# Gated layer of a fused attention and expert kernel: one of its seven outer products made by halves, inner products in sequence, some gates on ScalarE

## The chip, the cores and the metric

The kernel runs on one core of a Trainium2 chip. The metric is the device time of one execution in microseconds (us). The core has five engines that run side by side and wait for one another through semaphores: TensorE (PE in the profile; its weight loads are PEld), VectorE (DVE), ScalarE (ACT), GpSimd (POOL) and SyncE (SP). Every engine takes its own instructions in the order in which the program gives them.

## What is computed

The reference is an attention in which a query sees only the keys of its own hash bucket, followed by a two-layer block with a squared ReLU:

```python
batch, n_heads, seq, head_dim = (4, 8, 768, 64)
q_bits = (einsum('bhsd,dk->bhsk', q, proj) > 0)      # 6 bits; the same for k
mask = q_bucket[:, :, :, None] == k_bucket[:, :, None, :]
scores = where(mask, scale * q @ k.T, -1e9)
attn_out = softmax(scores) @ v
x = attn_out.transpose(0, 2, 1, 3).reshape(3072, 512)
h = x @ w_in                      # w_in 512 x 2048
r = maximum(h, 0.0)
g = r * r
out = g @ w_out                   # w_out 2048 x 512
```

Everything is float32. The change is in the two-layer block, above all in `h = x @ w_in` and the gate `g = max(h, 0) * h`.

## The kernel before

The block works on three chunks of 1024 rows (`NCHUNK` = 3). Both of its matrix products are made with Strassen's scheme in Winograd's form: each operand is cut into 2 x 2 blocks, and seven products of half-size blocks take the place of eight. `product` is that scheme for one block of weights. The weights' sums are kept in DRAM (`w_in_7`, and for the second level `w_in_49` and `w_out_49`); the sums of `x` are made on VectorE:

```python
def product(n, w, at, bt, c11, c12, c21, c22, hook=None):
    acc = [ps_m.tile([P, 512], FP32, name=f"acc{i}")[:, 0:w] for i in range(3)]
    ...
    add(0, at(0), bt["11"], True, False)
    one = keep(0, "one")              # ScalarE copy out of PSUM
    add(1, at(1), bt["21"], True, True)
    if hook:
        hook()
    c11(acc[1], one)
    add(0, at(4), bt["t2"], False, False)
    two = keep(0, "two")
    add(2, at(3), bt["t1"], True, False)
    five = keep(2, "five")
    add(0, at(5), bt["t3"], False, False)
    three = keep(0, "three")
    add(2, at(6), bt["22"], False, True)
    c12(acc[2], two)
    c22(three, five)
    add(0, at(2), bt["t4"], False, True)
    c21(acc[0])
```

An accumulator keeps adding after it has been copied, so the next product into the same bank must wait until the copy has been read out. `ps_m` has two buffers of each name (`acc0`, `acc1`, `acc2`) and `ps_t` has one (`acc3`, and `tp`)[...].

The first layer is made by `hidden` in chunk 0 (seven products, no second level) and by `hidden_pair` in chunks 1 and 2. A pair is two hidden units; each call of `hidden_pair` makes one half of it. Five of the seven outer products (each 128 x 512, over two blocks of features) are made whole in each half. The other two are made for both halves at once by a second level of the scheme, in seven inner products of 128 x 256 each, spread over the call in four steps:

```python
def hidden_pair(i, n, half):
    ...
    if half == 0:
        load_inner(i, n + 1)
        now[0], now[1] = (inner_steps(i, n, j) for j in range(2))
    *steps, put = now[half]
    add(0, 0, "11", True, False)
    one = keep(0, "one")
    if half:
        now[0][4](1, b11[:, r], one)
    else:
        steps[0]()
    add(2, 3, "t1", True, False)
    five = keep(2, "five")
    steps[1 - half]()
    add(0, 4, "t2", False, False)
    two = keep(0, "two")
    steps[2 - half]()
    if half == 0:
        put(0, b11[:, r], one)
    add(2, 6, "22", False, True)
    gate_sum(b12[:, r], acc[2], two)
    steps[3 - half]()
    if half:
        put(0, b21[:, n], now["three"])
    add(0, 5, "t3", False, True)
    three = keep(0, "three")
    gate_sum(b22[:, r], three, five)
    if half:
        steps[3]()
        put(1, b21[:, r], three)
    now["three"] = three
```

`gate_sum` and `put` are an addition and a gate on VectorE; the gate is one instruction (`max(h, 0) * h`). After each half come `minus(b_t[:, r], b12[:, r], b11[:, r])`, part of the sums that the second layer starts with (`inner_sums`), `minus(b12[:, r], b22[:, r], b12[:, r])`, and two maxima over `q` and `k` (`peak`).

The second layer, `project(i)`, makes seven outer products, each by seven inner ones. Before an inner product can use `t4`, a subtraction on VectorE must have made it in place. In chunk 0, four of the steps also make the second-level weights for the first layer of the later chunks, and the first of them loads the next chunk's `x` afterwards:

```python
def factor_units(n):
    src = [new_h()... for _ in range(2)]
    for j in range(2):
        nc.gpsimd.dma_start(out=src[j], in_=w_in_7[j * NQ + n, :, 5:7])
    sums = [new_h()... for _ in range(2)]
    sums_a(...)                       # four operations on VectorE
    for lo, hi, t in (...):
        nc.gpsimd.dma_start(out=w_in_49[n, :, :, lo:hi], in_=t)

for k in range(7):                    # in project(i)
    if i == 0 and k < NQ:
        factor_units(k)
    if k == 6 and more:
        load_inner(i + 1, 0)
    def hook():
        y21 = b[:, NQ:NR, 0:QN]
        minus(y21, y21, t2)           # t4
        if k + 1 < 7 and k not in (1, 3):
            inner_sums(k + 1)
        if k == 6 and more:
            sums_inner(i + 1)
    ...
    product(NQ, QN, a_with_load, bt, ..., hook)
    if k == 0 and i + 1 < NCHUNK:
        load_x(i + 1)                 # 2 MB, on GpSimd's queue
```

`new_h` turns through five buffers.

Of the kernel before, what the change touches and what calls it, by code (L numbers as in the profile page):

```python
# [34 lines left out]
def kernel(  # L35
# [10 lines left out]
    nc = tc.nc  # L46
# [37 lines left out]

    w_in_49 = p_d.tile([NQ, P, 2, 7, P], FP32, name="w_in_49")
    w_in_21 = p_d.tile([P, NFT // 2, HF], FP32, name="w_in_21")
# [419 lines left out]

    PLACE = 0, 5, 6, 1, 2, 3, 4

    def sums_a(a11, a12, a21, a22, s1, s2, s3, s4):
        nc.vector.tensor_tensor(out=s1, in0=a21, in1=a22, op=ALU.add)  # L510
        nc.vector.tensor_tensor(out=s3, in0=a11, in1=a21, op=ALU.subtract)
        nc.vector.tensor_tensor(out=s2, in0=s1, in1=a11, op=ALU.subtract)
        nc.vector.tensor_tensor(out=s4, in0=a12, in1=s2, op=ALU.subtract)

# [49 lines left out]
    def load_unit(n, pool=p_i):  # L564

        if n < NCHUNK * NR and n not in w_unit:
            r = order(n)
            w_unit[n] = pool.tile([P, 7, NFT // 2, P], FP32, name="w_unit", bufs=2 if pool is p_i else 1)
            m = 7 if n < NR else 5
            nc.sync.dma_start(out=w_unit[n][:, 0:m], in_=w_in_7[r, :, 0:m])  # L570

    def sum_x(i, n):
# [19 lines left out]
    with tc.manual_schedule():  # L592
# [173 lines left out]
        def guard():  # L766

            most = p_k.tile([1, 2], FP32, name="most")
            tp = ps_t.tile([P, 512], FP32, name="tp")
            for w in range(2):  # L770
                nc.tensor.transpose(
                    out=tp[0:1, w * P:(w + 1) * P], in_=top[:, w:w + 1], identity=ident
                )
            nc.vector.tensor_reduce(
                out=most, in_=tp[0:1, 0:2 * P].rearrange("o (w f) -> o w f", w=2), axis=AXL.X,
                op=ALU.max,
            )
            nc.vector.tensor_scalar(
                out=slow, in0=most[:, 0:1], scalar1=most[:, 1:2], scalar2=PLAIN / (scale * D),
                op0=ALU.mult, op1=ALU.is_gt,  # L780
            )
# [51 lines left out]
        def factor_units(n):  # L833

            src = [new_h().rearrange("p (a f c) -> p a f c", a=2, c=P) for _ in range(2)]
            for j in range(2):
                nc.gpsimd.dma_start(out=src[j], in_=w_in_7[j * NQ + n, :, 5:7])
            sums = [new_h().rearrange("p (a f c) -> p a f c", a=2, c=P) for _ in range(2)]
            sums_a(
# [3 lines left out]
            for lo, hi, t in (  # L843
                (0, 2, src[0]), (2, 3, src[1][:, :, 1:2]), (3, 5, sums[0]), (5, 7, sums[1])
            ):
                nc.gpsimd.dma_start(out=w_in_49[n, :, :, lo:hi], in_=t)

        def load_inner(i, n):

            if n < NQ:  # L850
                w_inner[i, n] = []
                for j, name in enumerate((("sum0", "sum3"), ("sum2", "sum1"))[n % 2]):
                    t = p_y.tile([P, 4, QN], FP32, name=name).rearrange("p a (b c) -> p (a b) c", c=P)
                    nc.sync.dma_start(out=t[:, 0:7], in_=w_in_49[n, :, j])
                    w_inner[i, n].append(t)

        def quarters_x(i, j):

            b = xs[i][0][:, 2:4, 0:HN] if j == 0 else xs[i][0][:, 0:2, HN:NCH]
            return b[:, 0, 0:QN], b[:, 0, QN:HN], b[:, 1, 0:QN], b[:, 1, QN:HN]  # L860

        def sums_inner(i):

            t_inner[i] = [p_y.tile([P, NQ, QN], FP32, name=f"t{m}", bufs=2) for m in range(2)]
            for j, t in enumerate(t_inner[i]):
                y11, y12, y21, y22 = quarters_x(i, j)
                minus(t[:, 0], y12, y11)
                minus(t[:, 1], y22, t[:, 0])
                minus(t[:, 2], y21, t[:, 1])
                minus(y12, y22, y12)  # L870

        def inner_steps(i, n, j):


            w, t = w_inner[i, n][j], t_inner[i][j]
            y11, t3, y21, y22 = quarters_x(i, j)
            hs = {}
            if i not in snaps:
# [4 lines left out]
            def mul(out, a, b, start, stop):  # L883
                nc.tensor.matmul(  # L884
                    out=out, lhsT=w[:, a], rhs=b, start=start, stop=stop, skip_group_check=True
                )

            def step_0():
                a0, a1 = (ps_m.tile([P, 512], FP32, name="acc1")[:, 0:QN] for _ in range(2))
                mul(a0, 0, y11, True, False)  # L890
                nc.scalar.copy(out=one, in_=a0)
                mul(a1, 1, y21, True, True)
                hs[0] = new_h()
                nc.vector.tensor_tensor(out=hs[0][:, 0:QN], in0=a1, in1=one, op=ALU.add)
                hs["a0"] = a0

            def step_1():
                hs["a2"] = ps_t.tile([P, 512], FP32, name="acc3")[:, 0:QN]
                mul(hs["a0"], 4, t[:, 1], False, False)
                nc.scalar.copy(out=two, in_=hs["a0"])  # L900
                mul(hs["a2"], 3, t[:, 0], True, False)
                nc.scalar.copy(out=five, in_=hs["a2"])

            def step_2():
                mul(hs["a0"], 5, t3, False, False)
                nc.scalar.copy(out=three, in_=hs["a0"])
                mul(hs["a2"], 6, y22, False, True)
                nc.vector.tensor_tensor(out=hs[0][:, QN:HN], in0=hs["a2"], in1=two, op=ALU.add)
                hs[1] = new_h()
                nc.vector.tensor_tensor(out=hs[1][:, QN:HN], in0=three, in1=five, op=ALU.add)  # L910

            def step_3():
                mul(hs["a0"], 2, t[:, 2], False, True)
                nc.scalar.copy(out=hs[1][:, 0:QN], in_=hs["a0"])

            def put(unit, out, other):
                h = hs[unit]
                nc.vector.tensor_tensor(out=h, in0=h, in1=other, op=ALU.add)
                gated(out, h)

            return step_0, step_1, step_2, step_3, put

        def hidden_pair(i, n, half):
# [4 lines left out]

            def add(to, a, b, first, last):
                for f in range(NFT // 2):  # L930
# [5 lines left out]

            def keep(of, name):
                t = p_r.tile([P, 512], FP32, name=name)
                nc.scalar.copy(out=t, in_=acc[of])
                return t  # L940

            if half == 0:
                load_inner(i, n + 1)
                now[0], now[1] = (inner_steps(i, n, j) for j in range(2))
            *steps, put = now[half]
            add(0, 0, "11", True, False)
            one = keep(0, "one")
            if half:
                now[0][4](1, b11[:, r], one)
            else:  # L950
                steps[0]()
            add(2, 3, "t1", True, False)
            five = keep(2, "five")
            steps[1 - half]()
            add(0, 4, "t2", False, False)
            two = keep(0, "two")
            steps[2 - half]()
            if half == 0:
                put(0, b11[:, r], one)
            add(2, 6, "22", False, True)  # L960
            gate_sum(b12[:, r], acc[2], two)
            steps[3 - half]()
            if half:
                put(0, b21[:, n], now["three"])
            add(0, 5, "t3", False, True)
            three = keep(0, "three")
            gate_sum(b22[:, r], three, five)
            if half:
                steps[3]()
                put(1, b21[:, r], three)  # L970
            now["three"] = three

# [4 lines left out]

        def inner_sums(k, n=slice(0, NQ)):

# [5 lines left out]
            y11, y12, y21, y22 = b[:, n, 0:QN], b[:, n, QN:HN], b[:, at, 0:QN], b[:, at, QN:HN]  # L985
            minus(t1, y12, y11)
            minus(t2, y22, t1)
            minus(y12, y22, y12)

# [64 lines left out]
        def project(i):  # L1054
# [60 lines left out]
            for k in range(7):  # L1115
                b = OUTER[k][1]
                t1, t2 = tens.pop(k)
                if i == 0 and k < NQ:
                    factor_units(k)
                if k == 6 and more:  # L1120
                    load_inner(i + 1, 0)
                at = lambda m, k=k: lambda n: leaves[k, m][:, n]
                bt = {
# [88 lines left out]
        for i in range(NCHUNK):  # L1212
            for s in range(NR):
# [3 lines left out]
                else:  # L1217
                    hidden_pair(i, s // 2, s % 2)
                minus(b_t[:, r], b12[:, r], b11[:, r])
                if i == 0 and r in WHEN:  # L1220
# [15 lines left out]
                if i > 0 and s % 2:  # L1236
                    inner_sums(0, slice(s // 2, s // 2 + 1))
                minus(b12[:, r], b22[:, r], b12[:, r])
                for n in range(2):
# [244 lines left out]
```

## Time and profile before

| | |
|---|---|
| device time, median of 3 | 879.97 us (879.5 to 882.57) |
| span of the profiled run | 877.9 us, 12130 instructions |
| granted TensorE clock, mean | 0.996 |
| attention (to the first product of the block) | 331 us |
| chunk 0: both layers | 331 to 513 us |
| chunk 1: first layer, second layer | 513 to 606, 606 to 691 us |
| chunk 2: first layer, second layer | 691 to 784, 784 us to the end |
| one gate, 128 x 512, on VectorE (96 of them) | 691 ns |
| one addition of 128 x 512, of 128 x 256, on VectorE | 685, about 420 ns |
| one copy out of PSUM of 128 x 512, of 128 x 256, on ScalarE | 585, about 375 ns |

The profile gives each engine's busy time, groups of equal instructions with the mean length of one and the idle time just before them, and the order of time of each engine with what ended a wait. "`<-PE acc L931`" after a number of us is a wait that a product of line 931 ended. Line numbers are those of the kernel before. A float32 matmul shows as two records on TensorE, so the counts there are twice those of the code. The ends of TensorE's records are modelled; the distance from one start to the next is what a product takes.

### The profile page before, as it was taken

How to read it: one execution, taken by the hardware profiler on the slowest of the kernel's cores; microseconds unless marked ns; L12 is line 12 of the kernel's file. 1: busy time of each engine (PE TensorE's matmuls, PEld its weight loads, DVE VectorE, ACT ScalarE, POOL GpSimd, SP SyncE). 2: the span in 40 equal slices, each digit the busy share in tenths (PEclk: the TensorE clock that was granted, in tenths of full speed). 3: DMA queues.
4: the chain of work that ended last, by engine and by line, in shares of the span. 5: the costliest groups of instructions: out<-in, count | busy, mean ns of one | idle time of the engine just before them, and what ended most of it. 6: DMA issues, size and time to landing. Idle time of an engine off the chain costs nothing.

```text
span 877.9 us, 12130 instructions
## 1 busy us (share of the span) xinstructions
PE 864.8 (99%) x4340; PEld 518.7 (59%) x4340; DVE 760.4 (87%) x1099; ACT 391.5 (45%) x673; POOL 107.0 (12%) x172
## 2 busy tenths in 40 slices
PE   8999999999999999999999999999999999999996
PEld 3444444444444444444688865556888755568885
DVE  5999999999999998888779968888889788888875
ACT  6988888888888852222211123332111233321110
POOL 2000000000000001554231011111000211110002
PEclk9999999999999999999999999999999999999998
DMA  9777967998788536999897764536756754355565
GB/s 176 142 149 134 233 153 156 188 253 225 179 176 225 156 105 213 299 267 283 292 353 239 181 160 168 173 118 222 285 151 187 167 165 155 124 167 154 158 175 105
DMA packets 224131, 167.09 MB, mean 190 GB/s; under 512 B 164448, under 2 KB 181344, under 8 KB 224064
## 3 DMA queue, kind: packets, MB, share of 16 engines
q1 hardware_dynamic: 189152, 87.19, 41.0%
q0 software_dynamic: 12528, 41.30, 15.2%
q10 hardware_dynamic: 22384, 37.76, 14.0%
q8 instruction: 36, 0.59, 0.3%
q14 instruction: 31, 0.25, 0.1%
HBM read 124.52 MB, written 41.68 MB: 189 GB/s over the span
## 4 chain that ended last, share of the span: by engine, by line
PE 95%; DVE 2%; ACT 1%; DMA 1%; issue 0%; ACTq 0%; DVEq 0%
PE acc L712 40%; PE st L396 17%; PE acc L931 16%; PE xo L438 14%; PE acc L884 6%; PE hash L346 2%; PE tot L455 1%; DVE total L428 1%; DMA k_nat<-in_k_dram 1%; ACT bits L356 1%; ACT e L413 0%; PE xo L477 0%; DVE x_t L493 0%; PE tp L309 0%; DVE recs L487 0%
## 5 line engine op out<-in xcount | busy, mean ns | idle before, releaser
L413 ACT ACTIVATE e<-st 128x1024 f32<-128x1024 f32 x192 | 145.1, 810 | 44.9 <-PE st L396 41.0
L396 PE MATMUL st<-feat,feat 64*128 64x512 f32 (+1 forms) x768 | 150.4, 483 | 0.0
L438 PE MATMUL xo<-e,v_nat 128*64 128x512 f32 (+1 forms) x768 | 134.8, 492 | 0.0
L712 PE MATMUL acc<-b,leaf 128*128 128x256 f32 x600 | 133.2, 379 | 0.7 <-issue 0.7
L712 PEld LDWEIGHTS acc<-b,leaf 128*128 128x128 f32 x600 | 113.8, 190 | 17.1 <-issue 1.7
L428 DVE TENSOR_TENSOR total<-total,e 128x1536 f32<-128x1536 f32 x64 | 112.4, 1757 | 8.2 <-ACT e L413 3.6
L438 PEld LDWEIGHTS xo<-e,v_nat 128*64 128x64 f32 x768 | 51.3, 136 | 82.2 <-issue 74.3
L931 PE MATMUL acc<-t_x,w_unit 128*128 128x512 f32 x192 | 90.2, 592 | 0.0
L396 PEld LDWEIGHTS st<-feat,feat 64*128 64x128 f32 x768 | 66.0, 188 | 33.0 <-issue 23.2
L712 PE MATMUL acc<-t,leaf 128*128 128x256 f32 x336 | 76.3, 380 | 0.0
L356 ACT ACTIVATE bits<-hash,lifts 32x384 bf16<-32x384 f32 x120 | 68.6, 572 | 2.3 <-PE hash L346 0.5
L712 PEld LDWEIGHTS acc<-t,leaf 128*128 128x128 f32 x336 | 63.6, 190 | 9.4 <-DVE t L516 0.5
L796 DVE SCALAR_TENSOR_TENSOR b<-h 128x512 f32<-128x512 f32 x96 | 65.7, 691 | 3.0
L396 PE MATMUL st<-bits,bits 64*128 64x256 bf16 (+1 forms) x384 | 63.1, 325 | 1.7 <-ACT e L413 1.2
L931 PE MATMUL acc<-x,w_unit 128*128 128x512 f32 x128 | 60.1, 592 | 0.0
L712 PE MATMUL acc<-x,w_unit 128*128 128x512 f32 x128 | 56.6, 594 | 0.0
L712 PE MATMUL acc<-b_t,leaf 128*128 128x256 f32 x240 | 53.8, 379 | 0.0
L931 PEld LDWEIGHTS acc<-t_x,w_unit 128*128 128x128 f32 x192 | 36.5, 190 | 28.9 <-issue 26.8
L719 ACT COPY two<-acc 128x256 f32<-128x256 f32 (+1 forms) x29 | 12.5, 431 | 87.9 <-PE acc L712 63.1
L719 ACT COPY one<-acc 128x256 f32<-128x256 f32 (+1 forms) x29 | 12.5, 431 | 85.1 <-PE acc L712 46.9
L712 PEld LDWEIGHTS acc<-b_t,leaf 128*128 128x128 f32 x240 | 45.5, 190 | 6.2
L396 PEld LDWEIGHTS <-bits 64*128 64x128 bf16 x384 | 23.5, 93 | 42.5 <-issue 38.4
(159 smaller groups left out, 1165.5 us busy)
## 6 DMA issues: line engine op xcount, KB each, us to landing
leaf<-w_out ACTq DMA_DIRECT2D x142, 256.0 KB, 3.1
w_unit<-w_in SPq DMA_DIRECT2D x16, 640.0 KB, 4.0
raw<-in_moe_w_in_dram SPq DMA_DIRECT2D x16, 512.0 KB, 5.6
raw<-in_moe_w_out_dram SPq DMA_DIRECT2D x16, 512.0 KB, 4.6
w_unit<-w_in SPq DMA_DIRECT2D x8, 896.0 KB, 8.1
w_out<-sums POOLq DMA_DIRECT2D x16, 448.0 KB, 6.8
sum<-w_in SPq DMA_DIRECT2D x16, 448.0 KB, 4.8
v_nat<-in_v_dram SPq DMA_DIRECT2D x16, 384.0 KB, 4.3
```

Source lines behind the costliest of these rows:

```text
L346: nc.tensor.matmul(out=banks[g * NR_B:(g + 1) * NR_B, h, 0:HS], lhsT=projs[rows], rhs=feat[pr, w][rows, c * HS:(c + 1) * HS], start=True, ...
L356: nc.scalar.activation(out=t[h * D:h * D + NR_B, c * HS:(c + 1) * HS], in_=hashed[pr, w][at, h, 0:HS], func=ACTF.Sign, scale=HUGE, bias=li ...
L396: nc.tensor.matmul(out=st[:, h, 0:hi - lo], lhsT=src[pr, 1][rows, key], rhs=src[pr, 0][rows, lo:hi], start=first, stop=not first,)
L413: nc.scalar.activation(out=e[:, :, lo:hi], in_=sts[i][:, :, 0:hi - lo], func=ACTF.Exp, scale=scale)
L428: nc.vector.tensor_tensor(out=totals[pr], in0=totals[pr], in1=weights[pr, kt][:, :, 0:S], op=ALU.add)
L438: nc.tensor.matmul(out=xo[h * D:(h + 1) * D, lo:hi], lhsT=nat[pr, "v_nat"][:, h, kt * D:(kt + 1) * D], rhs=weights[pr, kt][:, h, lo:hi], s ...
L455: nc.tensor.matmul(out=tot[g * 32:(g + 1) * 32, 0:HS], lhsT=ones, rhs=totals[pr][:, h, c * HS:(c + 1) * HS], start=True, stop=True,)
L712: nc.tensor.matmul(out=acc[to], lhsT=a(i), rhs=b(i), start=first and i == 0, stop=last and i == n - 1, skip_group_check=True,)
L719: nc.scalar.copy(out=t, in_=acc[of])
L796: nc.vector.scalar_tensor_tensor(out=out, in0=h, scalar=0.0, in1=h, op0=ALU.max, op1=ALU.mult)
L884: nc.tensor.matmul(out=out, lhsT=w[:, a], rhs=b, start=start, stop=stop, skip_group_check=True)
L931: nc.tensor.matmul(out=acc[to], lhsT=w[:, PLACE[a], f], rhs=bt[b](f), start=first and f == 0, stop=last and f == NFT // 2 - 1, skip_group_ ...
```

## The change

The outer product number 3 (`t1` with its weights), which was made whole in each half, joins the two that are made by halves: three of the seven now go through the second level. TensorE has four outer products a half left, and three inner schemes of seven products (`i2`, `i4`, `i6`) a pair. These no longer run side by side, one for each half: `i2` runs through the even half, `i6` begins in it and ends in the odd one, and `i4` runs in the odd one. Three of a pair's eight gates go to ScalarE, as a Relu and a Square (`put_act`). The aim is fewer products on TensorE, with VectorE relieved of some of what the new sums add.

What goes with it: the second-level weights of the third product are made in chunk 0 by `factor_units_s`, with its four sums on GpSimd and its transfers on GpSimd's queue; they are stored as a third part of `w_in_49` and read into the free slots 4 to 6 of `w_unit` (and one slot beside the inner weights); the sums of `x` for it are made by `sums_inner`; `acc3` gets two banks and `tp` none of its own; the differences `b_t` and `b12` are made once a pair, for both units. The diff, cut:

```diff
-    w_in_49 = p_d.tile([NQ, P, 2, 7, P], FP32, name="w_in_49")
+    w_in_49 = p_d.tile([NQ, P, 3, 7, P], FP32, name="w_in_49")
...
-            m = 7 if n < NR else 5
+            m = 7 if n < NR else 4
             nc.sync.dma_start(out=w_unit[n][:, 0:m], in_=w_in_7[r, :, 0:m])
+            if n > NR and r < NQ:
+                load_s1(n)
...
+        def factor_units_s(n):
+            src = new_h().rearrange("p (a f c) -> p a f c", a=2, c=P)
+            for j in range(2):
+                nc.gpsimd.dma_start(out=src[:, j], in_=w_in_7[j * NQ + n, :, 4])
+            sums = new_h().rearrange("p (a c) -> p a c", c=P)
+            sums_a(
+                src[:, 0, 0], src[:, 0, 1], src[:, 1, 0], src[:, 1, 1],
+                *(sums[:, j] for j in range(4)), engine=nc.gpsimd,
+            )
+            for lo, hi, t in ((0, 2, src[:, 0]), (2, 3, src[:, 1, 1:2]), (3, 7, sums)):
+                nc.gpsimd.dma_start(out=w_in_49[n, :, 0, lo:hi], in_=t)
...
+            def put_act(out, h):
+                nc.scalar.activation(out=h, in_=h, func=ACTF.Relu)
+                nc.scalar.activation(out=out, in_=h, func=ACTF.Square)
...
+            mul(0, 0, "11", True, False)
+            one = keep("one")
             if half:
-                now[0][4](1, b11[:, r], one)
+                put(b11[:, r], h2[1], one)
+                i6[2]()
+                inner_sums(0, slice(n, n + 1), (0,))
+
+                plus(now["h12"], h6[0])
+                h22 = new_h()
+                nc.vector.tensor_tensor(out=h22, in0=now["three"], in1=h6[0], op=ALU.add)
+                i4[0]()
+                put_act(b12[:, n], now["h12"])
             else:
-                steps[0]()
-            add(2, 3, "t1", True, False)
-            five = keep(2, "five")
-            steps[1 - half]()
-            add(0, 4, "t2", False, False)
-            two = keep(0, "two")
...
+                i2[0]()
+            mul(0, 4, "t2", False, False)
+            two = keep("two")
             if half:
+                i6[3]()
+                i4[1]()
+                put_act(b22[:, n], h22)
+            else:
+                i2[1]()
+            mul(2, 6, "22", True, True)
+            h12 = now["h12"] = new_h()
+            nc.vector.tensor_tensor(out=h12, in0=acc[2], in1=two, op=ALU.add)
             if half:
+                i4[2]()
+                put(b21[:, n], h4[0], now["three"])
+                plus(h12, h6[1])
+                put_act(b12[:, r], h12)
+            else:
+                i2[2]()
+                put(b11[:, r], h2[0], one)
+                i6[0]()
+            mul(0, 5, "t3", False, True)
+            three = now["three"] = keep("three")
+            if half:
+                i4[3]()
+                gate_sum(b22[:, r], three, h6[1])
+                put(b21[:, r], h4[1], three)
+            else:
+                i2[3]()
+                i6[1]()
...
                 if i == 0 and k < NQ:
                     factor_units(k)
+                    factor_units_s(k)
                 if k == 6 and more:
                     load_inner(i + 1, 0)
+                    if i == 0:
+                        load_s1(NR)
...
-                minus(b_t[:, r], b12[:, r], b11[:, r])
+                for m in [r] if i == 0 else [] if s % 2 == 0 else [r - NQ, r]:
+                    minus(b_t[:, m], b12[:, m], b11[:, m])
...
-                    inner_sums(0, slice(s // 2, s // 2 + 1))
-                minus(b12[:, r], b22[:, r], b12[:, r])
+                    inner_sums(0, slice(s // 2, s // 2 + 1), (1,))
+                for m in [r] if i == 0 else [] if s % 2 == 0 else [r - NQ, r]:
+                    minus(b12[:, m], b22[:, m], b12[:, m])
```

The four steps of an inner scheme are, in both kernels: step 0, products 0 and 1 and an addition on VectorE; step 1, products 4 and 3; step 2, products 5 and 6 and two additions; step 3, product 2. Product 1 goes into one `acc3` bank and products 3 and 6 into another (new; before, product 1 had a bank of `acc1`), the rest into an `acc1` bank, which ScalarE copies after each of them.

## The prediction

> **What bounds the kernel now.** I read the page's busy shares first, then the groups by shape, the busy time by stage, and last the order of time on each engine in the two stages that the diff touches.
>
> ```profile
> PE 864.8 (99%) x4340; PEld 518.7 (59%) x4340; DVE 760.4 (87%) x1099; ACT 391.5 (45%) x673; POOL 107.0 (12%) x172
> ...
> L712 PE MATMUL acc<-b,leaf 128*128 128x256 f32 x600 | 133.2, 379 | 0.7 <-issue 0.7
> ```
> TensorE is idle for 13.1 of 877.9 us. The group below it shows one idle spot of 0.7 us in the products of line 712; it returns below. By stage (length, then busy time and records of TensorE, weight loads, VectorE, ScalarE, GpSimd; clock, DMA share, GB/s):
>
> ```profile
> 536.60:559.80 23.20, 23.20 (x70) 12.91 (x69) 19.65 (x34) 7.81 (x19) 4.24 (x8) 1.00 0.50 165
> ...
> 606.30:691.06 84.76, 84.76 (x394) 74.41 (x393) 76.49 (x110) 11.65 (x32) 8.05 (x13) 1.00 0.70 207
> ```
> The first row is one pair of hidden units (chunks 1 and 2 have four each, eight in all), the second the second layer of chunk 1. TensorE never stops; VectorE is close behind, at 85% and 90%. So only less TensorE work can make this faster, and any new wait of TensorE is paid in full.
>
> How a product is handed over, in the order of time of a pair:
>
> ```profile
> 536.52 1.88 PE L931 MATMUL acc<-x,w_unit 128*128 128x512 f32 x4
> 538.44 0.58 ACT L939 COPY one<-acc 128x512 f32<-128x512 f32 x1 [1.29 <-PE acc L931]
> 538.92 0.38 ACT L891 COPY o<-acc 128x256 f32<-128x256 f32 x1
> ```
> A wide product (four records, each fp32 matmul being two) takes 1.72 us of TensorE to the next start at 538.24; the inner one, half as wide and deep, 0.43 (two records; 392 records of this width in 84.75 us in the chain). ScalarE starts its copy 0.2 after the product and moves on after 0.48.
>
> The second layer of chunk 0, on GpSimd's, VectorE's and TensorE's own order of time:
>
> ```profile
> 434.25 0.95 POOL L554 DMA_DIRECT2D x<-x_all  x1
> 435.01 1.28 POOL L837 DMA_DIRECT2D h<-w_in  x2
> 447.36 0.68 POOL L846 DMA_DIRECT2D w_in<-h  x1 [11.07 <-DMA h<-w_in]
> ```
> ```profile
> 448.12 0.43 DVE L510 TENSOR_TENSOR h<-h 128x256 f32<-128x256 f32 x1 [1.21 <-DMA h<-w_in]
> 449.59 1.22 DVE L516 TENSOR_TENSOR b<-b,t 128x1024 f32<-128x1024 f32 x1
> ```
> ```profile
> 450.91 1.32 PE L712 MATMUL acc<-b,leaf 128*128 128x256 f32 x5 [0.72 <-issue]
> ```
> The weight pieces for `factor_units(1)` are queued behind the 2 MB load of `x` and land 12 us later; VectorE waits for them, and only then does the `t4` subtraction of the running product (449.59 to 450.81). TensorE wants `t4` at 450.19 and stops until 450.91. **That is the 0.7 us of the page**: this chain has no slack now.
>
> [...]the trace has 585 for the copy out of PSUM and 631 for L161[...]. One table load stands in the program before and after.[...]
>
> **The change part by part.**
>
> *TensorE.* A pair had 20 matmuls of 512 (17.20 us at 0.86) and 14 of 256 (6.02); it gets 16 and 21: 13.76 + 9.03 = 22.79 for 23.22. Saved: 0.43 a pair, **3.4 us** over eight.
>
> *VectorE.* Per pair three more 256 additions (0.42), two more 512 additions (0.685), three gates fewer (0.691): +0.56, or 20.2 of 22.8 us. It fits in sum, so it is the order that decides.
>
> *ScalarE.* Two wide copies go, five inner copies and six activations of about 0.6 come: some 12 us of 22.8. Not full, but it now waits for VectorE in the middle of its queue.
>
> *A pair laid out by hand.* The odd half is `hidden_pair` with `half` = 1; times are us from its start, each step taken in the order in which its queue holds it. TensorE: product 0 to 1.72, `i6[2]` 2.58, `i4[0]` 3.44, `t2` product 5.16, `i6[3]` 5.59, `i4[1]` 6.45, `22` 8.17, then `i4[2]`. ScalarE's `one` is ready at 2.5. VectorE then does `put` 1.35, two additions 0.8, two differences 0.85, the sum into `h12` 0.65: done at 6.15. ScalarE, idle since 3.6, may only now start `put_act` (1.2, to 7.4); then `two` 0.5, `i6[3]` 0.38, `i4`'s `two` 0.38: 8.65. `i4[2]` needs that copy and could have started at 8.17: **0.5 us**. Next: `five` 9.0, the second `put_act` 10.2, `i4`'s `three` 10.55; VectorE: inner sum 11.0, `put` b21 12.35, `h12` 13.0; third `put_act` 14.25, `three` 14.75, `i4[3]` 15.1, and then `one` of the next pair, 15.65. TensorE had ended this half at 11.75 and wants to go on into that bank at 11.75 + 2.58 = 14.33: **1.4 us**. VectorE's tail (two gated sums, two `b_t`, one difference, two `b12`, two peaks: 7.5) runs from 14.9 to 22.3, then the first inner sum to 22.7. TensorE reaches `i6[0]` at 21.3 and needs the `acc3` bank this sum frees: **1.4 us**. Together 3.3 a pair; the first pair of a chunk has no tail before it, so 0.5: 2 x (0.5 + 3 x 3.3) = **20.8 us**.
>
> *Start of the second layer, chunks 1 and 2.* Before, VectorE's `t4` subtraction came at 613.46, 7.2 after the pairs' end, and TensorE wants it by 10.3 (six products of 1.72 come first). After: tail from 3.1, 7.5 long, 1.2 for itself: 11.8, a wait of 1.5; the next `t4` ended 0.5 before its need and inherits the lag: another 1.4. Twice 2.9: **5.8 us**.
>
> *Second layer of chunk 0.* `factor_units_s` puts between the stores of one step and what follows in GpSimd's queue: two loads (issue 1.1, landing 3.5), four operations (1.8), three stores (2.1), 8.5 us. The load of `x` moves from 434.3 to about 443, the loads behind it land at 455 to 456 for 448, sums to 457.5, `t4` to 458.7: TensorE waits 7.9 instead of 0.7. From then on a step of that chain takes stores 1.4, the 8.5, loads 1.4 and 4.3 to land, sums 1.45: 17 us for the 12.04 of a product. Steps 2 and 3 so wait some 5 each: 7.2 + 5.1 + 5.2 = **17.5 us**.
>
> The eight further subtractions in `sums_inner` lie where VectorE had slack (14.61 busy of 23.20 in a chunk's first pair). The extra slots of `w_unit` can go only after `i6[3]`, 5.6 into the odd half, and 640 KB landed in 3.9: hidden, with some 2 us to spare.
>
> Sum: -3.4 + 20.8 + 5.8 + 17.5 = +40.7, from 880: **about 921 us**.
>
> **The rivals.** *The waits are hidden and the saving is real*: 876.5. For it: VectorE and ScalarE have room in sum, and `acc3` gets two banks. Against it: three handovers of a pair run through two in-order queues, and the GpSimd chain has no slack. *Only GpSimd's chain hurts*, VectorE catching up in each pair: about 894. *Only the pairs hurt*, the small loads landing in the shadow of others: about 903.[...] *DMA*: the second layer of chunk 0 has 390 GB/s in its middle; if `x` takes longer for that, the chain gains a few us more.
>
> **Range and chances.** Hand layouts take each handover at its mean and may count a wait that is partly absorbed, so I set 916, under the sum. Low end 890: a third of the losses stays (44.1 / 3 - 3.4 = 11). High end 934: all of them and three tenths more (44.1 x 0.3 = 13 over the sum). Faster by 2% (under 862.4) can't come from 3.4 us. Within 2% reaches to 897.6 and takes either chain being mostly hidden: 0.24.
>
> **What would show it.** Right: gaps of 5 us or more in line 712's products in the second layer of chunk 0, each after a late `t4`, with VectorE waiting for the weight pieces; pairs of about 26 us in place of 23.2, ScalarE's Relu waiting for VectorE, TensorE waiting for ScalarE at a wide product and for VectorE at an inner one. TensorE's busy time lower by 3 to 4 us in any case. Wrong: pairs of 22.8 with no idle TensorE, or second-layer stages of unchanged length. Most likely error: the size of the VectorE lag that is carried from pair to pair.

## The result, and the profile after

The changed kernel takes **927.87 us** (median of five, 926.45 to 928.54) against 879.87 for the kernel before on the same chip: a ratio of 1.0538, 95% interval 1.0522 to 1.0554. The change costs 48 us. Line numbers below are those of the changed kernel: its line 721 is line 712 of before, 960 is 931 (wide products), 915 is 884 (inner products).

The page of the kernel after (busy shares, the granted clock in forty slices, the chain that ended last by engine, one group):

```profile
PE 873.5 (94%) x4388; PEld 530.1 (57%) x4388; DVE 768.6 (83%) x1123; ACT 421.4 (45%) x745; POOL 136.4 (15%) x208
...
PEclk9999999999999999999887999999999999999998
...
PE 79%; DVE 9%; ACT 5%; issue 4%; DMA 2%; ACTq 0%; POOL 0%; DVEq 0%; POOLq 0%
...
L721 PE MATMUL acc<-b,leaf 128*128 128x256 f32 x600 | 139.2, 390 | 27.1 <-issue 27.1
```

TensorE now stands still for 52.6 of 926.1 us (13.1 before), and its chain to the end, 95% TensorE before, has 9% of VectorE and 5% of ScalarE in it. The same group of 600 records of the second layer that stood 0.7 us before stands 27.1, and a record lasts 390 ns in the mean instead of 379. The clock row gives the reason for the longer records: it dips to 8, 8 and 7 tenths in three slices, from 440 to 510 us.

From the starts of each stage's first product, the 48 us divide as follows:

| stage | before, us | after, us | more, us | predicted |
|---|---|---|---|---|
| chunk 0, second layer | 85.7 | 113.9 | 28.2 | 17.5 |
| chunks 1 and 2, first layer | 92.8, 92.8 | 100.3, 100.2 | 14.9 | 17.4 (20.8 less 3.4) |
| chunk 1, second layer; chunk 2, second layer to the end | 84.7, 94.1 | 87.1, 96.9 | 5.1 | 5.8 |

**Chunk 0's second layer.** TensorE in order of time (start, length, what it made, how many records; in brackets the idle time before and what ended it):

```profile
464.01 3.75 PE L721 MATMUL acc<-b,leaf 128*128 128x256 f32 x8 [13.70 <-issue]
...
479.02 1.97 PE L721 MATMUL acc<-b_t,leaf 128*128 128x256 f32 x8 [0.18 <-issue]
...
500.51 8.45 PE L721 MATMUL acc<-b,leaf 128*128 128x256 f32 x24 [9.16 <-issue]
```

Three stops, 23.0 us in all: at the product that takes `t4`, in steps 1, 2 and 3. The first eight records after a long stop take 3.75 us, after a short one 1.97.

VectorE in the same stretch:

```profile
443.68 1.47 DVE L516 TENSOR_TENSOR t<-b_t 128x1024 f32<-128x1024 f32 x1
...
461.21 0.43 DVE L510 TENSOR_TENSOR h<-h 128x256 f32<-128x256 f32 x1 [13.27 <-DMA h<-w_in]
...
462.69 1.22 DVE L516 TENSOR_TENSOR b<-b,t 128x1024 f32<-128x1024 f32 x1
```

VectorE waits 13.27 us for the pieces of weights, makes the four sums, then `t4` (462.69 to 463.91), and TensorE goes on 0.1 later. Why the pieces are so late stands in GpSimd's order of time:

```profile
433.25 1.45 POOL L858 DMA_DIRECT2D w_in<-h  x2 [5.69 <-DVE h L512]
434.69 1.12 POOL L863 DMA_DIRECT2D h<-w_in  x2
439.91 1.69 POOL L510 TENSOR_TENSOR h<-h 128x128 f32<-128x128 f32 x1 [4.10 <-DMA h<-w_in]
441.58 2.49 POOL L511 TENSOR_TENSOR h<-h 128x128 f32<-128x128 f32 x1
444.03 1.43 POOL L512 TENSOR_TENSOR h<-h 128x128 f32<-128x128 f32 x1
...
448.43 0.76 POOL L554 DMA_DIRECT2D x<-x_all  x1
449.17 1.08 POOL L849 DMA_DIRECT2D h<-w_in  x2
...
467.77 0.45 POOL L510 TENSOR_TENSOR h<-h 128x128 f32<-128x128 f32 x1 [2.59 <-DMA h<-w_in]
```

The loads, the four sums and the stores of `factor_units_s` stand between the store of 433.25 and the load of `x`, which leaves at 448.43 instead of 434.3; the pieces behind it leave at 449.17 and land at 461. And a sum of 128x128 takes 1.69 and 2.49 us here, but 0.45 in the next step, where VectorE mostly waits.

The clock around the first stop (windows: length; busy time and records of TensorE, weight loads, VectorE, ScalarE, GpSimd; granted clock, DMA share, GB/s):

```profile
456.00:459.00 3.00, 0.00 (x0) 0.00 (x0) 0.00 (x0) 0.00 (x0) 0.00 (x0) 0.50 1.03 413
...
466.00:468.00 2.00, 2.00 (x7) 1.53 (x6) 0.49 (x2) 0.00 (x0) 0.23 (x1) 0.50 0.28 105
...
470.00:472.00 2.00, 2.00 (x11) 1.75 (x11) 0.00 (x0) 0.37 (x1) 2.00 (x5) 1.00 0.54 103
```

During the stop the clock falls to 0.50, and it stays there for about five more once products run again: 7 records in 2 us where 11 fit later. After the third stop it is 0.50 again, for about six. About half of those 11 us is lost, some 5.6.

**The pairs.** Windows of the first pair of chunk 1 and of the second, with the same columns:

```profile
541.60:564.88 23.28, 23.15 (x76) 13.91 (x75) 15.64 (x32) 9.60 (x23) 2.18 (x4) 1.00 0.54 156
564.88:590.34 25.46, 23.60 (x75) 13.83 (x74) 19.97 (x36) 11.56 (x27) 4.27 (x8) 1.00 0.47 158
```

A pair in the middle of a chunk takes 25.46 us for 23.2 before: TensorE stands still for 1.86 of them, although VectorE is busy for only 78% and ScalarE for 45%. Its handovers, on ScalarE, VectorE and TensorE:

```profile
565.86 0.63 ACT L979 ACTIVATE h<-h 128x512 f32<-128x512 f32 x1 [2.42 <-DVE h L972]
...
567.05 0.57 ACT L968 COPY three<-acc 128x512 f32<-128x512 f32 x1
...
567.78 0.60 ACT L968 COPY one<-acc 128x512 f32<-128x512 f32 x1
```
```profile
573.06 1.81 DVE L762 TENSOR_REDUCE peaks<-raw_qk 128x2 f32<-128x768 f32 x2
574.78 0.42 DVE L929 TENSOR_TENSOR h<-acc,o 128x256 f32<-128x256 f32 x1
```
```profile
568.44 1.98 PE L960 MATMUL acc<-t_x,w_unit 128*128 128x512 f32 x4 [0.82 <-ACT one L968]
...
575.26 0.70 PE L915 MATMUL acc<-t_x,w_unit 128*128 128x256 f32 x2 [0.96 <-DVE h L929]
```

ScalarE's third Relu waits 2.42 us for VectorE's sum. The copies of `three` and of an inner product were ready to be made, and that of the next pair's `one` soon after, but they stand behind it in the queue. TensorE needs the bank of `one` and stops. Some seven microseconds later it stops again, at `i6[0]`, for an inner sum that VectorE makes only after its peaks.

Both stops come six times, once in each pair but the first of a chunk. ScalarE's wait in the list of waits from 427 us on (total, times, longest):

```profile
ACT h L979 <- DVE h L972: 37.8, 15, 3.0
```

### The profile page after: what moved, and what is told of

Read it like the earlier page. It is cut to its first block, busy times and chain, and to the rows that moved or that the text cites. A ratio compares the mean times of both kernels' runs of the same rounds, so it can differ in the third digit from the quotient of the medians.

```text
span 926.1 us, 12380 instructions
## 1 busy us (share of the span) xinstructions
PE 873.5 (94%) x4388; PEld 530.1 (57%) x4388; DVE 768.6 (83%) x1123; ACT 421.4 (45%) x745; POOL 136.4 (15%) x208
## 3 DMA queue, kind: packets, MB, share of 16 engines
q10 hardware_dynamic: 22384, 37.76, 13.7%
## 4 chain that ended last, share of the span: by engine, by line
PE 79%; DVE 9%; ACT 5%; issue 4%; DMA 2%; ACTq 0%; POOL 0%; DVEq 0%; POOLq 0%
PE acc L721 38%; PE st L396 16%; PE xo L438 13%; PE acc L960 5%; PE acc L915 3%; DVE h L972 2%; DVE b L805 1%; PE hash L346 1%; DVE peaks L762 1%; PE tot L455 1%; ACT h L979 1%; ACT b L980 1%; DVE b_t L516 1%; DVE total L428 1%; DMA k_nat<-in_k_dram 1%
## 5 line engine op out<-in xcount | busy, mean ns | idle before, releaser
L721 PE MATMUL acc<-b,leaf 128*128 128x256 f32 x600 | 139.2, 390 | 27.1 <-issue 27.1
L721 PEld LDWEIGHTS acc<-b,leaf 128*128 128x128 f32 x600 | 116.7, 196 | 46.2 <-issue 29.8
L960 PE MATMUL acc<-t_x,w_unit 128*128 128x512 f32 x128 | 60.9, 599 | 4.9 <-ACT one L968 4.9
L728 ACT COPY two<-acc 128x256 f32<-128x256 f32 (+1 forms) x29 | 12.5, 432 | 85.5 <-PE acc L721 60.8
L805 DVE SCALAR_TENSOR_TENSOR b<-h 128x512 f32<-128x512 f32 x72 | 49.1, 691 | 2.2
L396 PEld LDWEIGHTS <-bits 64*128 64x128 bf16 x384 | 23.6, 93 | 42.6 <-issue 38.4
L1095 POOL DMA_DIRECT2D out_dram<-h x26 | 16.8, 655 | 182.7 <-DVE h L1088 181.2
```

Of the source, the lines that this page charges most:

```text
L396: nc.tensor.matmul(out=st[:, h, 0:hi - lo], lhsT=src[pr, 1][rows, key], rhs=src[pr, 0][rows, lo:hi], start=first, stop=not first,)
L721: nc.tensor.matmul(out=acc[to], lhsT=a(i), rhs=b(i), start=first and i == 0, stop=last and i == n - 1, skip_group_check=True,)
L805: nc.vector.scalar_tensor_tensor(out=out, in0=h, scalar=0.0, in1=h, op0=ALU.max, op1=ALU.mult)
L960: nc.tensor.matmul(out=acc[to], lhsT=w[:, PLACE[a], f], rhs=bt[b](f), start=first and f == 0, stop=last and f == NFT // 2 - 1, skip_group_ ...
L1095: queue.dma_start(out=out[at, m0 + a * 32:m0 + (a + 1) * 32].rearrange("(c i) j -> i c j", i=32), in_=ot[a * 32:(a + 1) * 32].rearrange("i ...
```

## The experiments

Each is the changed kernel with one edit, unless said otherwise; ratios are to the kernel before, with 95% intervals. The first four ask why chunk 0 lost 28 us and not 17.5, the next three what the order of the gates costs, the last three whether the idea pays once both are put right.

### The load of `x` on another queue

```diff
-                    load_x(i + 1)
+                    load_x(i + 1, nc.sync)
```

> The changed kernel, but the next chunk's x (2 MB) is asked for on SyncE's queue at the same place of the program, and not on GpSimd's ahead of the weight pieces of factor_units(1). Theory A (a queue on GpSimd, each step of it behind the one before): the pieces of step 1 need not wait for x, land some 4 us after their request at 448.4 and not 10.6, and the first long stop of TensorE in the second layer of chunk 0 goes from 13.7 to about 6 to 8 us; the second (9.2) stays; total about 919 to 922. Rival (the DMA engines themselves are full of x and of leaves, whichever queue asks): the pieces land as late as now, both stops stay, total 926 to 929.

Measured: 923.27 us, 1.0493 (1.0472 to 1.0514). TensorE's step 1:

```profile
459.33 3.67 PE L721 MATMUL acc<-b,leaf 128*128 128x256 f32 x8 [7.49 <-issue]
```

The stop falls from 13.70 to 7.49, so `x` ahead of the pieces of step 1 is worth 6.2 us of it. The edit does more than change the queue, however: on SyncE nothing holds the load up, and it leaves at 428.2, 20 us earlier than in the kernel after. So the run doesn't tell apart the order of GpSimd's queue and the load of the DMA engines. The total is 1.3 us above what was expected, since a step-0 product now waits 1.13 us for its leaf weights and step 2 stops 1.11. The stop of step 3, 8.83 for 9.16, doesn't care: the load is no part of it.

### The four GpSimd sums left out

This stores loaded pieces in the place of the sums: same transfers, same bytes, other contents, so the third part's weights are not those of the reference.

```diff
-            sums = new_h().rearrange("p (a c) -> p a c", c=P)
-            sums_a(..., engine=nc.gpsimd)
+            sums = src.rearrange("p a f c -> p (a f) c")
```

> The changed kernel without the four sums on GpSimd in factor_units_s: it stores the loaded pieces where the sums should be, so the output isn't the reference's. Loads and stores keep their number and bytes. It measures what the four operations (6.9 us in steps 0 and 2, 1.8 in steps 1 and 3) add to the queue. If the queue is one chain: first stop of TensorE 13.7 - 6.9 = about 7, second 9.2 - 6.9 = about 2 to 3, VectorE's 128x1024 subtractions at 1.22 us throughout, total about 911 to 914. Rival (the loads behind x set the step, the sums hide beside them): stops and total within 2 us of the changed kernel.

Measured: 911.9 us, 1.0363 (1.0343 to 1.0384). TensorE in steps 1 and 3, and VectorE in step 0:

```profile
458.30 3.61 PE L721 MATMUL acc<-b,leaf 128*128 128x256 f32 x8 [8.02 <-issue]
...
487.73 7.10 PE L721 MATMUL acc<-b,leaf 128*128 128x256 f32 x24 [3.37 <-issue]
```
```profile
443.38 1.22 DVE L516 TENSOR_TENSOR t<-b_t 128x1024 f32<-128x1024 f32 x1
```

The stops shrink by 5.7 and 5.8 us, most of the 6.9 us that the sums of steps 0 and 2 each lasted, and the whole by 16. VectorE's subtraction takes 1.22 us again, for the 1.47 of 443.68 above. The edit also takes one `h` buffer fewer in each step; but in the kernel after no load on GpSimd's queue waited for a buffer from 433 us on, so the gain doesn't come from there. Sixteen operations that the prediction counted as 0.45 us each are a third of the loss.

### `factor_units_s` three steps later

```diff
                 if i == 0 and k < NQ:
                     factor_units(k)
-                    factor_units_s(k)
+                if i == 0 and k >= NQ - 1:
+                    factor_units_s(k - NQ + 1)
```

> The changed kernel, but factor_units_s(n) is called in step n + 3 of chunk 0's second layer, and not in step n, so that no step's weight pieces queue behind it on GpSimd. Same work, same bytes. Theory A: both long stops of TensorE go (0 to 1 us left in step 1, as before the change), and with them the slow products after each stop: the stage takes about 86 us in place of 113.9, total about 899 to 901. Rival[...]: VectorE's subtractions are as slow in steps 3 to 6 and the stage loses 5 us or more there; total 904 or more.

Measured: 907.63 us, 1.031 (1.0293 to 1.0327); the stage takes 92.3 instead of 113.9. The stops of steps 1 to 3 are gone but for 0.99, so it is where this work stands in the queue, and not that it is done, that cost 22 us. The total is the one that the rival foresaw (904 or more), and VectorE's subtractions of 128x1024 beside the moved sums do take up to 1.48 us. But the hoped-for 86 was missed by a new wait. VectorE and TensorE, steps 5 and 6:

```profile
504.95 0.71 DVE L1088 STREAM_TRANSPOSE h<-o 128x512 f32<-128x512 f32 x1 [2.96 <-DMA w_in<-h]
```
```profile
516.37 3.75 PE L721 MATMUL acc<-b_t,leaf 128*128 128x256 f32 x8 [4.25 <-issue]
```

The transposes of the result take their buffers from the same five `h` buffers, and wait 2.96 and 3.73 us until the moved stores have left them; the seven slowed subtractions ahead of them lost some 1.5 us together.

### TensorE kept busy in the stops

Unused products of 128x512 are put ahead of the product that takes `t4`, fourteen in step 1 and nine in step 3. Nothing else is changed.

```diff
+            if filler:                    # 14 in step 1, 9 in step 3, of chunk 0
+                void = ps_t.tile([P, 512], FP32, name="acc3", bufs=2)
+                for _ in range(filler):
+                    nc.tensor.matmul(out=void, lhsT=ident, rhs=b11[:, 0], start=True, stop=True)
             add(0, at(2), bt["t4"], False, True)
```

> The changed kernel with 14 matmuls of 128x512 (result unused) on TensorE just before the last product of step 1 of chunk 0's second layer, and 9 before that of step 3, where it stands still for 13.7 and 9.2 us. After these stops the products ran slower for some 11 us each, at a granted clock of 0.73 to 0.77. If the stand-still is what lowers the clock: with the filler the clock stays at 1.0, the products after it take 1.72 us, and the total falls by 4 to 6 us, to 922 to 924, though TensorE does 20 us more work. Rival (the clock falls for another reason, power or the load of the DMA engines): products after the stops as slow as before, total 927 to 931.

Measured: 926.67 us, 1.0532 (1.0508 to 1.0557), not the 922 to 924 expected. The 11 us from 464.00 in this kernel's windows; in the kernel after they held 39 records at a mean clock of 0.77:

```profile
464.00:475.00 11.00, 11.00 (x52) 9.68 (x52) 2.35 (x7) 1.49 (x4) 5.38 (x11) 1.00 0.74 229
```

The clock stays at 1.00, and the eight records from 463.84 take 1.97 us where those from 464.01 took 3.75: it is the standing still that halves it, to 0.50 in the kernel after. Chunk 1 starts at 537.96 for 541.60, 3.6 us earlier, less than 5.6 because step 2 now stops 2.38 us and runs slowly after that. The two times, 924.72 and 928.62, don't settle the gain in the total.

### The gates behind the copies

The order on ScalarE's queue alone: each of the three `put_act` calls goes behind the next inner step, and so behind the copies of that place.

```diff
                 i4[0]()
-                put_act(b12[:, n], now["h12"])
...
                 i4[1]()
-                put_act(b22[:, n], h22)
+                put_act(b12[:, n], now["h12"])
...
                 i4[2]()
+                put_act(b22[:, n], now["h22"])
                 put(b21[:, n], h4[0], now["three"])
                 plus(h12, h6[1])
-                put_act(b12[:, r], h12)
...
                 i4[3]()
+                put_act(b12[:, r], h12)
```

> The changed kernel, but each put_act (Relu and Square on ScalarE) stands behind the copies out of PSUM that TensorE waits for: b12 of the first unit behind i4[1], b22 of the first unit behind i4[2], b12 of the second behind i4[3]. Same instructions. Theory B (ScalarE, waiting for VectorE at the Relu, holds up the copies behind it): the stops at i4[2] (0.3 us) and at the next pair's second product (0.8 to 1.0) go, the keep of three comes 3 us sooner, and VectorE's tail reaches the next pair earlier, leaving 0 to 0.9 of the stop at i6[0]; pairs 22.8 to 23.7 in place of 25.46; total 914 to 918. Rival (VectorE's sum of work is the bound in the pairs, at 20 of 25.5 us plus handovers): pairs stay at 25 or more, total 925 to 929.

Measured: 906.52 us, 1.03 (1.0283 to 1.0318). The window of chunk 1's four pairs:

```profile
542.78:634.57 91.79, 91.79 (x297) 55.74 (x296) 75.04 (x137) 46.02 (x105) 14.94 (x28) 1.00 0.55 175
```

No stop is left in the pairs, and at the `t4` products of chunks 1 and 2 only one of 0.40 us, although VectorE and ScalarE do the same work. 21.4 us come back, more than expected: the stop at `i6[0]`, of which I had left up to 0.9 to VectorE's load, goes too. VectorE was late there because it had itself waited for copies (14.7 us for `three` in the kernel after) that stood behind a Relu that waited for VectorE.

### Only the third gate moved

> The changed kernel with only the third put_act (b12 of the second unit) moved behind i4[3]; the other two stay. The prediction gave its delay to the keep of three as the cause of two stops: at the next pair's second product (now 0.8 to 1.0) and, through VectorE's tail, at i6[0] (1.0 to 1.1). If so, both go and the 0.3 at i4[2] stays: pairs 22.9 to 23.4, total 908 to 912. Rival (the earlier two hold up just as much): pairs 24 or more, total 915 or more.

Measured: 913.21 us, 1.0375 (1.0357 to 1.0393). The two larger stops of a pair are gone. What is left in the last pair of chunk 1:

```profile
632.52 1.13 PE L915 MATMUL acc<-x,sum 128*128 128x256 f32 x4 [0.69 <-ACT o L934]
```

So one call, the third `put_act`, makes both stops and 14.7 of the 21.4 us. The first two make the stop at `i4[2]` and the rest. The total is 1.2 us above what was expected, and the mean pair, 23.6, is 0.2 above.

### The three gates back on VectorE, at the same places

```diff
             def put_act(out, h):
-                nc.scalar.activation(out=h, in_=h, func=ACTF.Relu)
-                nc.scalar.activation(out=out, in_=h, func=ACTF.Square)
+                gated(out, h)
```

> The changed kernel with its three ScalarE gates back on VectorE as one instruction each, at the same places. ScalarE then never waits for VectorE, VectorE has 2.07 us more a pair (22.0 of 22.8). Theory B (order of the queues): the stops at i4[2] and at the next pair's second product go, but VectorE's tail ends later in the next pair, so the stop at i6[0] grows from 1.0 to some 2.5 to 3; pairs 25.3 to 26, total 926 to 932. Rival (the sum of VectorE's work binds): no stop at i6[0] alone but all through the pair, pairs of 27 or more, total 938 or more.

Measured: 913.69 us, 1.0385 (1.0366 to 1.0404), faster than either theory allowed. Pairs take 23.71, with one stop:

```profile
574.89 0.70 PE L915 MATMUL acc<-t_x,w_unit 128*128 128x256 f32 x2 [0.56 <-DVE h L929]
```

VectorE with all gates is 0.56 late; with three fewer it was 0.96 late. Both theories took VectorE's load as the cause; most of the loss is the back-and-forth between two in-order queues. As the change places them, gates on ScalarE cost 14.2 us.

### Both put right

The order of the gates as above; the third part's weights made in steps 3 and 4 from buffers that are free there, their pieces loaded a unit ahead, plain copies from device memory to device memory; transfers moved to match.

```diff
-                    factor_units_s(k)
+                if i == 0 and k == 3:
+                    for n in range(NQ):
+                        copy_pieces(n)        # by SyncE, DRAM to DRAM
+                    load_pieces(0); load_pieces(1)
+                    factor_units_s(0)
+                if i == 0 and k == 4:
+                    for n in range(1, NQ):
+                        if n + 1 < NQ:
+                            load_pieces(n + 1)
+                        factor_units_s(n)
```

> The changed kernel with the Relu and Square behind the copies (as in e4_act_late), and with the third part of the weights made in steps 3 and 4 of chunk 0's second layer out of a buffer that is free there (that of the maxima, whose first loads move behind the stage) and not out of the five h buffers; the three pieces that are only copied go from DRAM to DRAM, the next pieces are asked for ahead of the sums, and that chunk's out stores go by SyncE. If both theories hold and nothing else is hidden: no stop of TensorE over 1.5 us, chunk 0's second layer 86 to 88 us, pairs about 22.95, total 877 to 880, so level with the kernel before or up to 0.3% faster. Rival (sums on GpSimd slow VectorE's subtractions wherever they run): the stage takes 90 us or more and the total stays above 882.

Measured: 885.37 us, 1.0059 (1.0046 to 1.0073), not the 877 to 880 expected. TensorE at the first pair of chunk 1:

```profile
520.46 1.49 PE L924 MATMUL acc<-x,sum 128*128 128x256 f32 x4 [4.11 <-DMA sum<-w_in]
```

The stage of chunk 0 takes 86.9 us, as expected. The inner weights, read on SyncE's queue, now come late: that queue has been given the copies and the stores of the result. The stop and the products behind it, slowed at a clock of 0.50 from 522 to 524 us, make the first layer of chunk 1 97.8 us long, where that of chunk 2 takes 91.8. The next kernel tests this by taking both transfers off the queue.

### Both put right, transfers back on GpSimd's queue

The kernel just shown, with the copies on GpSimd's queue beside each step and the stores of the result left where the change has them.

> e10_mended with its two leftovers taken away: there the first inner weights of chunk 1 came 4.1 us late, because the out stores that had moved to SyncE stood ahead of them, and the plain copies went out at once beside the 2 MB load of x and held up a leaf by 0.8. Here the out stores are back on GpSimd's queue, and each copy goes with its own step's pieces. If these two are all that was left: no stop over 1 us but the known 0.7 of step 1 (and that after the last output), total 878.5 to 881, level with the kernel before at 879.9; the saving on TensorE of 3.4 us would show as 1 to 3. Rival (VectorE, slowed by GpSimd's sums in steps 3 to 5, is late again at the end of the stage): a stop of 2 us or more there, total above 882.

Measured: 880.31 us, 1.0008 (1.0000 to 1.0016). The 4.11 us stop is gone; which of the two transfers had made it was not separated. The kernel is level with the one before, not faster, and 47.6 us ahead of the change. Its chunk 0 stage is 85.5 us, the 85.7 of before. In the kernel just shown seven of the sixteen sums on GpSimd still took 1.31 to 1.44 us each; here TensorE's only stop in that stage is the 0.70 of step 1. The window of its second pair in chunk 1:

```profile
537.08:560.05 22.97, 22.97 (x75) 13.89 (x74) 19.78 (x36) 11.98 (x28) 4.26 (x8) 1.00 0.53 175
```

A pair is 22.97 where the matmul count says 22.79 and before took 23.2: nearly half of the saving goes in small delays of about 0.1 us at two handovers. Two stops, 0.52 and 0.40 us, take 0.9 of the 2 us left. TensorE's last product still starts 0.5 us before its time in the kernel before, and the transfers behind it end at the same 877.9.

### The same order, gates on VectorE

The kernel of "Both put right" with `put_act` as `gated`.

> e10_mended with the three gates back on VectorE at the mended places. It asks whether ScalarE's gates are needed at all once the order is right. If VectorE at 22.0 of 22.8 us a pair is enough: total within 2 us of e10_mended. If its tail lands too late for the acc3 bank at i6[0]: a stop of 1 to 3 us in all but the first pair of a chunk, total 8 to 20 us over e10_mended.

Measured: 897.4 us, 1.0197 (1.0177 to 1.0218), 12 us above it. TensorE's waits from 500 us on:

```profile
PE acc L924 <- DVE h L938: 7.0, 6, 1.2
```

Here VectorE is the one that is late, 1.16 us in each later pair. Of the 12 us, some 2 lie in chunk 0, where none of these gates stand. So in the right order the gates on ScalarE earn about 10 us; at the places of the change they cost 14.

## Why the prediction was right, and where it was not

The time, 927.87, lies in the range (890 to 934), 7 us above the worked sum and 12 above the 916 named. Two of its three sums held, and were 3 us too high together; the third was 11 us short. That the total came out so near is in part luck.

**The pairs: right in size and place.** 14.9 measured for 17.4. The first pair's stop was set at 0.5, and 23.28 is 0.49 over the 22.79 of its matmuls, 0.3 of it at `i4[2]`. In later pairs, from start to start, the stop for `one` was 0.98 for 1.4 (the 0.82 in the bracket counts from the modelled end of the product before), at `i6[0]` 1.12 for 1.4, at `i4[2]` 0.3 for 0.5 (0.9 in the last pair of a chunk). The reason given, VectorE's sum in the middle of ScalarE's queue, is what the late gates show. Copies that were ready to be made stood up to 3.0 us behind a Relu that was not. The stop at `i6[0]` is as laid out too: VectorE's tail, 7.1 us for 7.5, starts when the copy of `three` has come, and moving behind that copy the one call that stood ahead of it on ScalarE removes the stop. It was my later expectations that gave a part of it to VectorE's load.

**The starts of the second layer: right.** 5.1 for 5.8; stops of 0.70 and 1.27 in chunk 1, of 1.01 and 1.27 in chunk 2, at the `t4` products as told.

**Chunk 0: the mechanism right, the size wrong.** 28.2 for 17.5. The chain of GpSimd's queue, the load of `x`, the pieces, `t4` and TensorE is as laid out. Two terms of the sum were off, besides a slip (`t4` at 458.7 for a need at 450.19 is a wait of 8.5, not 7.9, so that the terms laid out come to 18.1):
- "Four operations (1.8)" was an estimate; the trace of before has only one form of GpSimd sum, 128x32, at 241 ns. They were 6.9 us in steps 0 and 2, 1.8 in step 1 and 2.9 in step 3. `x` so left at 448.4 and not at 443, and step 1 stopped 13.7 instead of 7.9. Leaving the sums out brings that stop to 8.0, where the layout without their 1.8 would say 6.7. What these sums and VectorE's subtractions cost each other was the missing term: 1.32 to 2.50 us for a sum that takes 0.45 alone, 1.47 for a subtraction that takes 1.22.
- No term stood for the clock: 5.6 us of products slowed at 0.50.

"Steps 2 and 3 so wait some 5 each" was right only as a sum, 0.18 and 9.16. The chain's steps took 15.0 us (464.0 to 479.0) and 21.5 (to 500.5) for the 17 laid out. The short one has quick GpSimd sums, and the halved clock used up most of its surplus; the long one has slow sums.

**TensorE's busy time "lower by 3 to 4 us in any case": wrong.** It rose from 864.8 to 873.5. Busy time counts length, and at the halved clock eight records of 128x256 count 3.75 us for 1.97. The saving itself exists: four pairs without a stop take 91.79 for 92.84, 1.0 us a chunk for the 1.7 worked out.

What stays open: whether the remaining 0.1 us delays at handovers of the last version can be had back by another order. It was not tried.

## What to carry to other kernels

Work moved to an idle engine is cheap only if the order of its queue is right: an operation that waits for a second engine must stand behind the copies that a third engine's banks depend on, or two half-empty engines wait for each other in turn, which took 21.4 us here. On a kernel with one engine at 99%, put a side job's place in the queue, and the buffers it shares, ahead of its amount: the same weights cost 28 us in steps 0 to 3 and nothing measurable in steps 3 and 4. And size a stop with what follows it: here TensorE's stops of 13.70 and 9.16 us were paid once more in 5 and 6 us of products at a clock of 0.50.

## What the runs showed of the hardware that I had not expected

**GpSimd's sums and VectorE's subtractions lengthen each other.** In the kernel after, a GpSimd sum of 128x128 with both inputs in SBUF takes 0.45 us with VectorE idle, as the prediction estimated, and 1.32 to 2.50 us in steps 0 and 2, while VectorE works on two SBUF inputs; its operations of 128x1024 then take up to 1.47 instead of 1.22. Each of the eight sums of these steps ends 0.31 or 0.32 us after the VectorE operation that was running when it started: the one of 444.03 at 445.46, behind a subtraction from 443.68 to 445.15. So each of these short sums cost what was left of the VectorE operation.

**A stop halves the clock.** In the kernel after, the granted clock is 0.50 from 455.5 to 469.0 us and from 496.5 to 506.6, around the ends of the stops of 13.70 and 9.16 us, and 1.00 between and up to the next stage. In the experiments the windows show 0.50 behind stops of 4.25 us ("`factor_units_s` three steps later", 516 to 520), 4.11 ("Both put right", 522 to 524) and 3.37 ("The four GpSimd sums left out", 490 to 492). Behind stops of 0.91 to 2.08 us eight records take 1.96 to 1.99 us, the full length. Of two stops of 2.38 us, each ahead of eight records, only one brought slow ones (first the kernel with unused products, then that of "The same order, gates on VectorE"):

```profile
478.55 3.51 PE L721 MATMUL acc<-b_t,leaf 128*128 128x256 f32 x8 [2.38 <-issue]
```
```profile
444.26 1.99 PE L721 MATMUL acc<-b,leaf 128*128 128x256 f32 x8 [2.38 <-DMA leaf<-w_out]
```

What tells the two apart was not shown. Once products ran again, the half lasted 5.0 and 6.1 us in the kernel after. In the kernel with unused products it was some 3, an estimate from its mean clock of 0.57 from 478 to 480 us, 0.58 from 480 to 482 and 1.00 from there on.
